# Logits' update as the first step of the next search, the second search held behind the first tokens, and the last block's results copied by ScalarE

## The chip, the cores and the metric

The kernel runs on one core of a Trainium2 chip. The metric is the device time of one execution, in microseconds (us). Engines are named as the profile names them: PE (TensorE), DVE (VectorE), ACT (ScalarE), POOL (GpSimd), SP (SyncE); PEld is PE's weight load. Each engine works through its own queue in order; SP's and POOL's queues also issue the DMA transfers.

## What is computed

Three layers follow one another. Attention with 4 sink positions and a window of 128 gives 3072 tokens of 512 channels. A dense layer (512 to 2048 to 512, with a piecewise quadratic activation) follows. Then each token goes to one of eight experts: all 3072 x 8 logits are taken from the greatest down, and a token takes an expert if the token is free and the expert has fewer than 384 tokens:

```
logits = x @ w_gate
flat = logits.flatten()
order = np.argsort(-flat)
for idx in order:
    tok, e = (int(idx) // E, int(idx) % E)
    if assigned[tok] >= 0 or counts[e] >= cap:
        continue
    assigned[tok] = e
    counts[e] += 1
for e in range(E):
    mask = assigned == e
    h = np.maximum(x[mask] @ w1[e], 0.0)
    out[mask] = h @ w2[e]
```

All matrix work is done in split precision: every operand is a high part (names ending in `h`) and a remainder (ending in `l`), and a product is three matmuls.

## The kernel before, in words

**Stages.** Attention and the dense layer run block by block (256 tokens each) up to about 866 us. The change touches what comes then: routing and the eight experts, and the end of the last block of the dense layer.

**Routing.** The logits stand in one tile `logits` (128 partitions x 24 x 8). Routing goes expert by expert in eight phases (`phase`, L760). A phase finds the expert that fills up first among those left, and its 384 tokens. `prep` (L765) takes each token's greatest logit `v` and its one-hot `own`. `search(r)` (L775), seven rounds, finds the threshold bit by bit: DVE compares `v` with 32 candidate thresholds (`ind`), PE counts (`pg`, copied by DVE as `cnt`, then `pc`), DVE turns the counts into the next candidates (`hit`, `row`, `m`, `th`). `pick` (L822) names the expert (`pe` on PE, `top`, `eid`, `est` on DVE); SP reads `eid` and can then load that expert's weights. `rank` (L854) numbers its tokens and, at its end (L869 to L876), updates the logits for the next phase: the expert found and the tokens taken are set to a very low value (`pe`, `pt`, and two writes of `logits`). `places` (L878) and `tokens` (L896) make one-hots (`oh`), PE adds them up to token numbers (`pk`), ACT and DVE finish them (`tf`, `tok`). `gather` (L944) has POOL issue three indirect transfers that fetch 128 token rows each (`xg`). `turn` (L957) transposes them on PE (`xt`); ACT writes the high part `xsh`, DVE the remainder `xsl`.

**Experts.** `weights` (L919) loads one of four chunks of `w1` and `w2` (SP, buffers `w1r`, `w2r`, four in all), ACT rounds them (`w1h`, `w2h`), and the remainder comes from DVE (`w1l`) or from ACT and an accumulating transfer on POOL's queue (`w2l`). `expert` (L967) has 96 matmuls `hp` (hidden layer, 384 tokens wide) and 72 `us` (output): 168 in all. After each hidden tile ACT writes `hh` and DVE `hl`. ACT copies the outputs (`ot`), POOL scatters them. In what follows, a place in an expert is the number of its 168 matmuls that stand ahead of it in PE's queue.

**What sets the order.** `experts` (L1039) gives every step a planned time; the steps are written in the order of these times, and the tile framework's scheduler puts the instructions of each engine in a fixed order by priority, in which the steps of `find` (prep, searches, pick, rank) rank as urgent (L1031). The instructions wait for one another through semaphores; an engine that waits holds all that is queued behind.

**The last block.** In `moe1_steps` (L601) the last block's outputs are left for after its logits; `done` (L674) copies each half tile from PSUM to `ev`, the low half by ACT, the high half by DVE (L686), and SP stores `ev` to `x2d`, from which the gathers read.

## Time and profile before

| | us |
|---|---|
| median of three runs | 1244.58 (1243.54 to 1244.86) |
| the profiled execution, its own time | 1243.53 |
| its span, first to last instruction | 1241.3 |
| PE busy | 1143.8 (92%) |
| DVE busy | 860.0 (69%) |
| ACT busy | 695.6 (56%) |
| POOL busy | 462.0 (37%) |
| mean granted clock of PE, share of full | 0.965 |

Times in the rows count from the span's start. A row of a timeline gives start, duration, engine, line, operation, tiles and shapes; in brackets how long the engine had been idle before it and who ended that. A row "x5" is five instructions merged. Matmuls overlap their neighbours, so their cost is read from start to start; the chain of waits has that already.

### The profile page before, as it was taken

Reading aid. Unit: us, or ns where it says so; the run is one execution under the profiler, and the core shown is the slowest. Engines: PE = TensorE matmul, PEld = TensorE weight load, DVE = VectorE, ACT = ScalarE, POOL = GpSimd, SP = SyncE. Lnnn points to the kernel's source line nnn. Section 1 sums busy time; section 2 is a strip of 40 time slices with the busy share of each in tenths; the row PEclk is TensorE's granted clock in tenths of the full one; section 3 lists DMA queues with packets and bytes.
Section 4 is the critical chain, followed back from the end, with each engine's and each line's share of the span. In section 5 each row is a group of like instructions: output and inputs, shape, how many; then the busy total and the mean of one; then the engine's idle time right before and its main releaser. Section 6 shows DMA issues by size and latency. Waiting matters only on the chain.

```text
span 1241.3 us, 24035 instructions
## 1 busy us (share of the span) xinstructions
PE 1143.8 (92%) x8444; PEld 1058.0 (85%) x8444; DVE 860.0 (69%) x2637; ACT 695.6 (56%) x1607; POOL 462.0 (37%) x574
## 2 busy tenths in 40 slices
PE   5998988999999999999999999999599999999995
PEld 3778878999999999999999999998478777778894
DVE  7798988677667777666777677656778677775310
ACT  5675557566667666666666666641454344444421
POOL 1245635344444444443445344440221222222210
PEclk9799989999999999999999999999699999999998
DMA  3555322112121112111111112000895577668620
GB/s 93 146 163 160 119 57 65 41 31 58 35 53 32 24 48 59 35 35 35 24 48 40 50 35 53 1 18 2 224 250 164 168 204 205 187 175 242 160 68 29
DMA packets 147715, 112.84 MB, mean 91 GB/s; under 512 B 101888, under 2 KB 126464, under 8 KB 147584
## 3 DMA queue, kind: packets, MB, share of 16 engines
q1 hardware_dynamic: 138992, 81.31, 22.7%
q0 software_dynamic: 8592, 29.89, 10.3%
q8 instruction: 69, 1.13, 0.4%
q14 instruction: 62, 0.51, 0.1%
HBM read 80.76 MB, written 13.11 MB: 76 GB/s over the span
## 4 chain that ended last, share of the span: by engine, by line
PE 40%; issue 11%; DMA 8%; DVE 8%; POOL 6%; ACT 6%; SPq 0%; POOLq 0%; DVEq 0%; ACTq 0%
PE hp L616 12%; PE up L641 12%; DMA w2r<-in_moe_w_dram 5%; PE us L1009 4%; PE hp L983 3%; DMA w2l<-w2r 3%; PE tp L365 2%; PE xp L384 2%; ACT pr L332 1%; ACT u L625 1%; PE sc L327 1%; POOL xa L403 1%; PE sc L328 1%; DVE ks L292 1%; DVE u L624 1%
## 5 line engine op out<-in xcount | busy, mean ns | idle before, releaser
L628 POOL TENSOR_TENSOR gl<-u,gh 128x256 fp32r<-128x256 f32 x192 | 146.5, 763 | 246.7 <-ACT gh L627 207.6
L641 PE MATMUL up<-woh,gl 128*128 128x256 f32 x576 | 169.9, 295 | 0.5 <-POOL gl L628 0.5
L641 PE MATMUL up<-woh,gh 128*128 128x256 f32 x576 | 165.7, 288 | 0.0
L641 PE MATMUL up<-wol,gh 128*128 128x256 f32 x576 | 165.4, 287 | 0.0
L625 ACT ACTIVATE u<-u,half 128x256 f32<-128x256 f32 x192 | 97.6, 509 | 98.5 <-DVE u L624 94.4
L616 PE MATMUL hp<-xh,wil 128*128 128x256 f32 x768 | 132.6, 293 | 4.6 <-ACT xh L404 3.0
L616 PE MATMUL hp<-xl,wih 128*128 128x256 f32 x768 | 127.1, 286 | 0.8 <-POOL xl L405 0.5
L616 PE MATMUL hp<-xh,wih 128*128 128x256 f32 x768 | 125.7, 285 | 0.0
L626 DVE TENSOR_TENSOR u<-hp,u 128x256 f32<-128x256 f32 x192 | 81.0, 422 | 46.7 <-ACT u L625 43.9
L616 PEld LDWEIGHTS hp<-xh,wil 128*128 128x128 f32 x768 | 107.8, 193 | 6.3 <-ACT xh L404 3.6
L641 PEld LDWEIGHTS up<-woh,gl 128*128 128x128 f32 x576 | 111.0, 193 | 1.7 <-POOL gl L628 0.9
L641 PEld LDWEIGHTS up<-woh,gh 128*128 128x128 f32 x576 | 110.8, 192 | 0.0
L641 PEld LDWEIGHTS up<-wol,gh 128*128 128x128 f32 x576 | 110.7, 192 | 0.0
L616 PEld LDWEIGHTS hp<-xl,wih 128*128 128x128 f32 x768 | 107.1, 192 | 1.8 <-POOL xl L405 1.8
L616 PEld LDWEIGHTS hp<-xh,wih 128*128 128x128 f32 x768 | 107.2, 193 | 0.8 <-issue 0.8
L624 DVE TENSOR_SCALAR u<-hp 128x256 f32<-128x256 f32 x192 | 80.8, 421 | 30.0 <-PE hp L616 26.3
L332 ACT ACTIVATE pr<-pr,sm 128x288 f32<-128x288 f32 (+1 forms) x160 | 85.4, 535 | 20.2 <-DVE sm L330 19.8
L627 ACT CAST gh<-u 128x256 fp32r<-128x256 f32 x192 | 77.5, 404 | 32.5 <-DVE u L626 30.2
L941 POOL DMA_DIRECT2D w2l<-w2r x32 | 29.5, 922 | 155.3 <-ACT w2l L939 138.8
L346 POOL TENSOR_TENSOR pr<-pr,sm 128x576 f32<-128x576 f32 x56 | 65.1, 1162 | 54.4 <-DVE sm L338 40.2
L991 DVE SCALAR_TENSOR_TENSOR hl<-hp,hh 128x384 fp32r<-128x384 f32 x64 | 35.4, 553 | 65.3 <-ACT hh L990 65.2
L1009 PE MATMUL us<-w2h,hl 128*128 128x512 f32 x192 | 79.5, 414 | 0.0
(273 smaller groups left out, 3096.6 us busy)
## 6 DMA issues: line engine op xcount, KB each, us to landing
w1r<-in_moe_w_dram SPq DMA_DIRECT2D x32, 512.0 KB, 5.7
w2r<-in_moe_w_dram SPq DMA_DIRECT2D x32, 512.0 KB, 5.3
w2l<-w2r POOLq DMA_DIRECT2D x32, 512.0 KB, 5.6
dr<-in_moe_w_in_dram SPq DMA_DIRECT2D x16, 512.0 KB, 3.8
dr<-in_moe_w_out_dram SPq DMA_DIRECT2D x16, 512.0 KB, 3.8
x2d<-ev SPq DMA_DIRECT2D x26, 256.0 KB, 2.0
kr<-in_k_dram SPq DMA_DIRECT2D x56, 96.0 KB, 2.6
vr<-in_v_dram SPq DMA_DIRECT2D x56, 96.0 KB, 2.2
```

What stands on the lines that cost most here:

```text
L332: nc.scalar.activation(pr, pr, AF.Exp, bias=sm[:, 0, u:u + 1], scale=-1.0, accum_out=sm[:, 1, u:u + 1])
L346: nc.gpsimd.tensor_tensor(out=pr, in0=pr, in1=r.unsqueeze(2).to_broadcast([P, 2, 2 * P + NS]), op=OP.mult)
L616: nc.tensor.matmul(ps, w_[:, k, fs], x_[:, k, :], start=(i == 0 and k == 0), stop=(i == 2 and k == 3))
L624: nc.vector.tensor_scalar(u, ps, -1.0, 1.0, op0=OP.max, op1=OP.min)
L625: nc.scalar.activation(u, u, AF.Square, bias=self.half, scale=0.5)
L626: nc.vector.tensor_tensor(out=u, in0=ps, in1=u, op=OP.max)
L627: nc.scalar.copy(gh, u)
L628: nc.gpsimd.tensor_tensor(out=gl, in0=u, in1=gh.bitcast(F32), op=OP.subtract)
L641: nc.tensor.matmul(o, g_[:, ts], self.w_out_part(w_, f)[:, cs], start=(f == fa and i == 0 and (cs.start > 0 or t == 0)), stop=(f == fz - 1 ...
L983: nc.tensor.matmul(ps, w_[:, k, fs], x_[:, k, :], start=(i == 0 and k == 0), stop=(i == 2 and k == 3))
L991: nc.vector.scalar_tensor_tensor(hl, ps, 0.0, hh.bitcast(F32), op0=OP.max, op1=OP.subtract)
L1009: nc.tensor.matmul(us[j], h_[:, o], w_[:, f % 2, :], start=(f == 0 and i == 0), stop=(f == nf - 1 and i == 2))
```

## The change

Three things. The update of the logits leaves `rank` and becomes a function `retire`, which the next phase's `prep` calls first. For the first phase, the first instruction of `retire` may stand in DVE's queue only behind the last `xsl` of the first tokens (an order, no semaphore). And the last block's high halves are copied by ACT instead of DVE.

```diff
@@ moe1_steps, done
                 nc.scalar.copy(ev[:, :hw], lo)
-                nc.vector.tensor_copy(ev[:, hw:], hi)
-                if not hold:
+                if hold:
+
+                    nc.scalar.copy(ev[:, hw:], hi)
+                else:
+                    nc.vector.tensor_copy(ev[:, hw:], hi)
                     nc.vector.tensor_copy(o, lg)
@@ phase
-    def phase(self, last, out):
+    def phase(self, last, out, before):
...
         def prep():
+            if before:
+                before["retire"]()
...
-            if not last:
-                pt = self.rw.tile([P, GT], F32, name="pt")
-                pe = self.rw.tile([P, E], F32, name="pe")
-                nc.vector.tensor_scalar(pe, st["est"], 2.0 * DEAD, -DEAD, op0=OP.mult, op1=OP.add)
...
+        def retire():
+
+            ge = st["ge"]
+            pt = self.rw.tile([P, GT], F32, name="pt")
+            pe = self.rw.tile([P, E], F32, name="pe")
+            got = nc.vector.tensor_scalar(pe, st["est"], 2.0 * DEAD, -DEAD, op0=OP.mult, op1=OP.add)
+            if not before:
+
+                self.tc.add_manual_dep(got.ins, out["turned"], AFTER, reason="behind the tokens")
...
+        out["retire"] = retire
@@ turn
-        nc.vector.tensor_tensor(out=xl[:, :, o], in0=ps, in1=xh[:, :, o].bitcast(F32), op=OP.subtract)
+        got = nc.vector.tensor_tensor(out=xl[:, :, o], in0=ps, in1=xh[:, :, o].bitcast(F32), op=OP.subtract)
+        cur["turned"] = got.ins.name
@@ experts
-            find, fetch = self.phase(k + 1 == E, curs[k])
+            find, fetch = self.phase(k + 1 == E, curs[k], curs[k - 1] if k else None)
```

`AFTER` is a dependency without a semaphore. The scheduler works the order of all engines out anew, so the instructions move in places that the diff doesn't name. Lines of the changed kernel are 1 to 15 higher than those of the kernel before.

**DVE, first phase, from the one-hots' inputs on.** Before (`ind`, `own`, `cnt`, `hit` are the second search's first round; `v` its prep):

```order
L876 TENSOR_TENSOR logits<-logits,pt 128x192
L885 SCALAR_TENSOR_TENSOR a<-a,z 128x24
L890 TENSOR_TENSOR rr<-bs,t_row 128x3x24
L767 TENSOR_REDUCE v<-logits 128x24
L887 TENSOR_SCALAR ab<-a 128x24
L781 TENSOR_TENSOR ind<-v,pat_11516 128x768
L769 TENSOR_TENSOR own<-logits,v 128x192
L900 TENSOR_TENSOR oh<-slot,ab 128x128x6 x2
L789 CAST cnt<-pg 128x32
L900 TENSOR_TENSOR oh<-slot,ab 128x128x6
L803 TENSOR_SCALAR hit<-pc 128x8
L900 TENSOR_TENSOR oh<-slot,ab 128x128x6
```

In the changed kernel:

```order
L899 SCALAR_TENSOR_TENSOR a<-a,z 128x24
L904 TENSOR_TENSOR rr<-bs,t_row 128x3x24
L901 TENSOR_SCALAR ab<-a 128x24
L914 TENSOR_TENSOR oh<-slot,ab 128x128x6 x4
L923 SCALAR_TENSOR_TENSOR tok<-pk,tf 128x3
L979 TENSOR_TENSOR xsl<-xt,xsh 128x4x128 x3
L881 TENSOR_SCALAR pe<-est 128x8
L887 TENSOR_TENSOR logits<-logits,pe 128x192
L888 TENSOR_TENSOR logits<-logits,pt 128x192
L773 TENSOR_REDUCE v<-logits 128x24
L787 TENSOR_TENSOR ind<-v,pat_11516 128x768
L775 TENSOR_TENSOR own<-logits,v 128x192
```

The one-hots, `tok` and the three `xsl` now stand together; the update and the whole second search stand behind them, among the first expert's `w1l` and `hl`. On PE the second search's pick moves from behind 50 of the first expert's matmuls to behind 126; on POOL the three gathers move ahead of the first `w2l` transfer.

**ACT, from the second expert's first weights to its tokens.** Before:

```order
L990 ACTIVATE hh<-hp 128x384
L935 CAST w1h<-w1r 128x1024
L939 ACTIVATE w2l<-w2r 128x1024
L940 CAST w2h<-w2r 128x1024
L907 COPY tf<-pk 128x3
L935 CAST w1h<-w1r 128x1024
L990 ACTIVATE hh<-hp 128x384
L939 ACTIVATE w2l<-w2r 128x1024
L940 CAST w2h<-w2r 128x1024
L935 CAST w1h<-w1r 128x1024
L990 ACTIVATE hh<-hp 128x384
```

In the changed kernel:

```order
L921 COPY tf<-pk 128x3
L1029 COPY ot<-us 128x512
L949 CAST w1h<-w1r 128x1024
L953 ACTIVATE w2l<-w2r 128x1024
L954 CAST w2h<-w2r 128x1024
L978 CAST xsh<-xt 128x4x128 x2
L949 CAST w1h<-w1r 128x1024
L953 ACTIVATE w2l<-w2r 128x1024
L978 CAST xsh<-xt 128x4x128
L954 CAST w2h<-w2r 128x1024
L1005 ACTIVATE hh<-hp 128x384 x6
```

Before, the first expert's last two `hh` stand between the second expert's late weight casts; in the changed kernel all eight stand ahead of the second expert's first cast, and the late casts stand ahead of that expert's `xsh` instead.

## Rows read from the trace of the kernel before

**Rows 1.** Busy time by stretch: stretch, its length, busy us (count) by engine, clock, DMA.
```profile
866.00:888.00 22.00, 10.04 (x96) 7.74 (x94) 17.72 (x75) 6.42 (x10) 5.07 (x5) 0.61 0.64 171
888.00:938.00 50.00, 46.04 (x286) 38.12 (x287) 36.43 (x123) 27.30 (x36) 12.34 (x12) 0.90 0.86 236
938.00:982.00 44.00, 41.90 (x290) 34.33 (x289) 32.89 (x118) 18.95 (x27) 10.21 (x10) 1.00 0.62 183
...
1157.00:1194.00 37.00, 37.00 (x207) 33.04 (x206) 9.18 (x15) 15.80 (x25) 9.06 (x10) 1.00 0.53 131
```
**Rows 2.** PE's waits, 888 to 1157 us: total us, times, longest.
```profile
PE pg L786 <- DVE ind L781: 6.9, 7, 2.3
PE pc L793 <- DVE cnt L789: 5.7, 6, 1.7
PE po L857 <- DVE tot L852: 2.6, 1, 2.6
```
**Rows 3.** Timeline of DVE, first search to first tokens.
```profile
844.25 0.35 DVE L767 TENSOR_REDUCE v<-logits 128x24 f32<-128x192 f32 x1
...
866.99 0.16 DVE L835 TENSOR_REDUCE top<-sm 128x1 f32<-128x8 f32 x1
...
867.76 0.42 DVE L686 COPY ev<-up 128x256 f32<-128x256 f32 x1
...
871.87 0.43 DVE L876 TENSOR_TENSOR logits<-logits,pt 128x192 f32<-128x192 f32 x1
...
873.97 0.55 DVE L900 TENSOR_TENSOR oh<-slot,ab 128x768 bf16<-128x768 bf16 x1
...
878.71 0.15 DVE L909 SCALAR_TENSOR_TENSOR tok<-pk,tf 128x3 int32<-128x3 f32 x1
```
**Rows 4.** Timeline of ACT, the same stretch.
```profile
867.97 0.65 ACT L685 COPY ev<-up 128x256 f32<-128x256 f32 x2 [23.85 <-PE up L641]
...
873.63 1.03 ACT L940 CAST w1h<-w1r 128x1024 fp32r<-128x1024 f32 x1
...
877.26 0.15 ACT L907 COPY tf<-pk 128x3 f32<-128x3 f32 x1
```
**Rows 5.** Timeline of POOL, the same stretch.
```profile
876.74 0.89 POOL L941 DMA_DIRECT2D w2l<-w2r  x1 [1.55 <-ACT w2l L939]
879.15 1.09 POOL L951 DMA_INDIRECT xg<-x2d,tok  x1 [1.52 <-DVE tok L909]
```
**Rows 6.** DMA issues, 866 to 890 us: queue, count, size, median us to landing.
```profile
x2d<-ev SPq DMA_DIRECT2D x2, 256.0 KB, 4.4
...
w2l<-w2r POOLq DMA_DIRECT2D x1, 512.0 KB, 4.6
```
**Rows 7.** Chain of waits: start, us, what.
```profile
888.09 3.58 PE hp L983 x11
...
896.62 0.47 DVE hl L991
...
919.64 5.65 DMA w2r<-in_moe_w_dram
...
929.77 2.40 PE us L1009 x10
...
943.16 2.46 PE hp L983 x13
```
**Rows 8.** Timeline of PE, the second expert's first matmuls.
```profile
938.40 0.87 PE L983 MATMUL hp<-xsh,w1l 128*128 128x384 f32 x4
```
**Rows 9.** Timeline of DVE, second search.
```profile
890.11 1.23 DVE L936 TENSOR_TENSOR w1l<-w1r,w1h 128x1024 fp32r<-128x1024 f32 x1 [0.16 <-ACT w1h L935]
...
891.87 0.19 DVE L789 CAST cnt<-pg 128x32 f16<-128x32 f32 x1 [0.53 <-PE pg L786]
...
896.44 0.18 DVE L789 CAST cnt<-pg 128x32 f16<-128x32 f32 x1
...
906.37 0.15 DVE L835 TENSOR_REDUCE top<-sm 128x1 f32<-128x8 f32 x1
```

More of the change, by code (lines that the diff above doesn't have):

```diff
@@ L17 @@
 DRAM = bass.MemoryType.DRAM
+AFTER = mybir.DependencyInfo(mybir.DependencyClass.NoSync, mybir.DependencyReason.DATA)
 DEP = mybir.DependencyInfo(mybir.DependencyClass.Sync, mybir.DependencyReason.DATA)
@@ L868, in rank @@
                 nc.vector.tensor_scalar(ge[:, i], z, float(P * i), None, op0=OP.is_gt)
-            if not last:
-                pt = self.rw.tile([P, GT], F32, name="pt")
-                pe = self.rw.tile([P, E], F32, name="pe")
-                nc.vector.tensor_scalar(pe, st["est"], 2.0 * DEAD, -DEAD, op0=OP.mult, op1=OP.add)
-                nc.vector.tensor_tensor(out=pt, in0=ge[:, 0], in1=ge[:, 3], op=OP.subtract)
-                nc.vector.tensor_scalar(pt, pt, 2.0 * DEAD, -DEAD, op0=OP.mult, op1=OP.add)
-                nc.vector.tensor_tensor(out=lm, in0=lm, in1=pe.unsqueeze(1).to_broadcast([P, GT, E]), op=OP.min)
-                nc.vector.tensor_tensor(out=lm, in0=lm, in1=pt.unsqueeze(2).to_broadcast([P, GT, E]), op=OP.min)
+        def retire():
[5 more added lines that the diff above has]
+                self.tc.add_manual_dep(got.ins, out["turned"], AFTER, reason="behind the tokens")
+            nc.vector.tensor_tensor(out=pt, in0=ge[:, 0], in1=ge[:, 3], op=OP.subtract)
+            nc.vector.tensor_scalar(pt, pt, 2.0 * DEAD, -DEAD, op0=OP.mult, op1=OP.add)
+            nc.vector.tensor_tensor(out=lm, in0=lm, in1=pe.unsqueeze(1).to_broadcast([P, GT, E]), op=OP.min)
+            nc.vector.tensor_tensor(out=lm, in0=lm, in1=pt.unsqueeze(2).to_broadcast([P, GT, E]), op=OP.min)
+        out["retire"] = retire
         def places():
```

## The prediction

> **What bounds the kernel now.** I read the views in this order: busy time by stretch, the matrix engine's waits, then the chain and the timelines around the place that the change touches. [Rows 1] cut the end of the program near the first hidden matmul of each expert (of four stretches like that from 938 one stands there): between 866 and 888 us there is almost no matmul work to do, the first expert takes 50 us, the ones after it about 44, and the seventh, beside which no search runs, takes 37. So two things cost time here: the hand-over from routing to the first expert, and what the search for the next expert costs beside each expert. A search's own matmuls are small: seven rounds of count matmuls. The larger part is in [rows 2]: between 888 and 1157 us PE stood still 6.9 us for `ind`, 5.7 us for `cnt` and 2.6 us for `tot`, all made by DVE for the search, 15.2 us together. DVE is late there because it works in order and the search's instructions stand behind `w1l` and `hl`, which wait for weights that are loaded only once the search before has named the expert. PE and DVE are thus tied to the load chain after each pick.
>
> **Term 1, the hand-over.** The pick is known at 866.99 (`top`); the first one-hot `oh` starts only at 873.97 and `tok` at 878.71 [rows 3]. In between DVE did five instructions of the logits' update, the first step and round 0 of the second search, and two 0.42 us copies `ev`; all of these leave that stretch. The first chain alone then needs some 4.5 us from `top` to `oh` and 2.1 us for four `oh`, so the one-hots end near 873.7 and the last six `pk` matmuls near 874.3. ACT is then the last: `tf` stands behind `w1h`, which runs from 873.63 to 874.66, since its weights had to land [rows 4]. `tf` no longer stands behind the `w2` pair, though, as it did at 877.26. So `tok` comes at 874.87, and with the 0.44 us from `tok` to the gather in [rows 3, 5] the first gather starts at 875.3 instead of 879.15. That is 3.8 us earlier. The `w2l` transfer of 876.74 now goes behind the gathers on POOL's queue [rows 5]; it goes out after three gathers, near 880, and with its 4.6 us [rows 6] lands near 885, while the first product that reads it stands 36 matmuls into the expert, after 891, which hides it. The two `ev` halves that move to ACT put four copies where two took 0.65 [rows 4]: the second store goes out about 0.5 us later on SP's queue, and `w2r` behind it; its 4.4 us landing [rows 6] ends by 874.3, 1 us before the gather that waits for it, so I cost it at nothing; without that cover it would cost up to 0.5. The `xsl` remainders no longer wait behind a search's `ind`, 0.4 us. The first hidden matmul moves from 888.09 [rows 7] to 883.9: **4.2 us earlier**.
>
> **Term 2, the first expert with a search inside it.** The second search used to run from 872 to 906.37 [rows 9], its first three rounds inside the hand-over where PE was idle. Now DVE's queue holds it until the third `xsl`, about 884.6. No row shows a search that begins there, so I bound it. Below: the first search, with nothing else on DVE, took 22.7 us from `v` to `top` [rows 3]; with some 0.9 us of the update in front (two `logits` like the 0.43 us one of 871.87, and `pe`) the pick would be at 908.2. But the order puts the pick behind 126 expert matmuls (50 before), 90 `hp` of 0.189 us and 36 `us` of 0.24 us [rows 7], 25.7 us together, which with 1.4 us of slow clock and 2.5 us of count matmuls is not before 913.5. Above: two rounds 4.57 us apart, as between 891.87 and 896.44 [rows 9], in all seven rounds plus 2.2 us give 918.8. I take the first search plus what DVE's order puts inside it, three `w1l` of 1.23 [rows 9] and seven `hl` of 0.47 us [rows 7]: 22.7 + 0.9 + 3.7 + 3.3 = 30.6, a pick at **915.2**, nearest to the row with an expert running. It is 8.8 us later than 906.37.
>
> **Term 3, the gap before the second expert.** From the pick the second expert's tokens need their own path, and in the new order ACT makes the casts of the second expert's `w1h`, `w2l`, `w2h` chunk 3 and half of chunk 4 before its `xsh`. In the kernel before the third `w2r` went out 13.3 us after the pick and landed 5.65 later [rows 7], because its buffer is freed by the first `w2l`. So: 18.9 us to that landing, 0.45 for an `ot` copy now ahead of it, 2.0 for `w2l` and `w2h`, 1.1 for two `xsh`, 1.95 for the next casts and 0.6 for the last `xsh`: 25.0 us. The first expert's 42 matmuls left after the pick last only some 10 us, so PE has nothing for most of the rest. The second expert's first matmul comes at 940.2 instead of 938.40 [rows 8]: **1.8 us later**, terms 1 and 2 included.
>
> PE starts that expert after a pause. After the like pause at 866 to 888 the granted clock was 0.61 of full [rows 1], which mixes the 2.4 GHz before with the 1.2 GHz after, and the first eleven hidden matmuls took 3.58 us, 0.325 each, against 0.189 later [rows 7]. Eleven at that rate cost **1.4 us** more. The Trainium skill, "TensorE: Matmul & The Clock Gate", Part 1, says that the slow clock is the array's default and only activity releases it, which speaks against any change that opens a pause; this case's trace agrees with its 0.325 us. Without that rule, had the clock stayed up, the sum below would end 1.4 us lower.
>
> **Term 4, what later experts give back.** The picks of the third to the seventh search move from 33, 21, 3, -12 and -22 matmuls into an expert to 68, 55, 37, 16 and -2. The load chain of a pick blocks ACT some 19 to 25 us after it. Before, `hh` casts of the running expert stood behind those late casts, so `hl`, and the search's `cnt` behind it on DVE, were late, and PE with them. In the new order the second expert's `hh` all stand ahead of the late casts, the third's all but one. Of the 15.2 us in [rows 2] 11.8 fall after 938. They could all go (-11.8) or, since `cnt` still stands behind late `w1l`, none (0). Of the experts two to five, two lose their `hh` behind late casts, two keep some; I take half, **5.9 us back**. The move of DVE's two copies in the last block saves nothing else: DVE is not waited for there.
>
> **Sum.** +1.8 + 1.4 - 5.9 = -2.7. The profiled execution took 1243.53 us (span 1241.3); it becomes 1240.8. The median of the runs, 1244.58, lies 1.05 above it, so the forecast is 1241.9. Its own range, with the second search one round faster or slower and a third to two thirds given back, is 1238 to 1246.
>
> **Rivals.** *The gap is not paid back (slower).* Each round in the first expert takes the 4.57 us of [rows 9] instead of about 4; the pick is then at 918.8, 3.6 later, and PE pauses as much longer; the second expert, whose rounds are also placed among its matmuls, gives nothing back, so only half of some 7 us returns: 3.2 + 3.6 - 3.4 = +3.4, about 1248. It decides once the second pick is later than about 918. For it: the order ties every round to a number of matmuls, and DVE's queue holds three `w1l` that wait for weights. Against it: the loads of that expert also start 3.6 us earlier. Chance 0.28.
>
> *The late waits vanish (much faster).* If the later picks free PE of all of the 11.8 us, 3.2 - 11.8 = -8.6, about 1236. For it: ACT's order in the second expert; against it: fourth and fifth experts keep `hh` behind late casts. Chance 0.19.
>
> *Earlier start and gap cancel (no change).* The tokens come 4.2 us earlier, the gap takes it, and later experts wait as before, only at other matmuls; or the gathers still wait for the stores and nothing is gained in front. +1.8 at most, 1244 to 1246. Chance 0.09.
>
> **Chances.** The forecast has 0.44, of which 0.27 lies below -0.2%, 0.15 within and 0.02 above; 0.2% is about what a measurement of this kernel can tell from no change. Faster 0.27 + 0.19 = 0.46; within 0.15 + 0.09 = 0.24; slower 0.02 + 0.28 = 0.30. Both signs hold much, so the range reaches over the rivals: 1234 to 1250.
>
> **What would show it.** Right: first gather at 875 to 876, first hidden matmul near 884; second pick 913 to 917; a pause of PE of 10 us or more before the second expert, with a granted clock below 1 there; second expert near 940; experts three to six each 1 to 2 us shorter than before, with less waiting for `ind` and `cnt`. Wrong, if the first gather is not 3 us earlier, if the pick comes after 918, or if PE's waits for DVE after 940 do not fall.

## The result and the profile after

The changed kernel is slower. Its median is 1256.2 us (1251.4 to 1260.2, six runs) against 1244.25 (1240.3 to 1248.8, six runs) for the kernel before, measured beside it; the ratio is 1.0071, with a 95% interval from 1.0043 to 1.0099. The profiled execution took 1254.8 us (span 1253.0, mean granted clock 0.961). Here and below a ratio is of fast runs alone; a run that is over 1.5% above the fastest of its kernel counts as slow, which leaves out five of twelve in experiment 12, the traced one among them, and one each in experiments 9 and 13.

Busy time by stretch, changed kernel, cut at the first hidden matmul of each expert (the columns are those of [rows 1]):

```profile
866.00:885.30 19.30, 7.79 (x58) 6.55 (x56) 8.69 (x36) 7.08 (x12) 5.18 (x5) 0.66 0.69 181
885.30:944.00 58.70, 46.31 (x308) 37.96 (x308) 42.31 (x144) 26.61 (x36) 13.74 (x13) 0.85 0.74 205
944.00:993.00 49.00, 44.71 (x287) 37.04 (x288) 33.39 (x120) 19.42 (x27) 9.94 (x10) 0.93 0.62 167
993.00:1036.60 43.60, 41.91 (x288) 34.42 (x287) 33.04 (x121) 19.17 (x27) 10.54 (x10) 1.00 0.63 181
1036.60:1080.50 43.90, 41.57 (x288) 34.25 (x287) 33.04 (x121) 19.28 (x27) 10.31 (x10) 1.00 0.63 177
1080.50:1126.80 46.30, 43.67 (x289) 35.63 (x288) 33.57 (x122) 19.18 (x27) 9.69 (x10) 0.96 0.62 172
1126.80:1166.40 39.60, 37.74 (x211) 32.96 (x210) 26.04 (x85) 21.84 (x31) 11.37 (x11) 1.00 0.87 248
1166.40:1203.40 37.00, 37.00 (x206) 32.83 (x205) 9.06 (x15) 15.50 (x24) 9.46 (x10) 1.00 0.62 158
```

Against [rows 1]: the hand-over is shorter (19.3 us instead of 22.0), the first expert longer (58.7 instead of 50), and the second longer (49.0 instead of 44) at a lower clock. The seventh takes 37 as before. The same view of the kernel before for the third to sixth expert, which [rows 1] leave out:

```profile
982.10:1027.10 45.00, 42.09 (x289) 34.16 (x288) 32.68 (x122) 18.88 (x27) 9.69 (x10) 1.00 0.63 178
1027.10:1070.60 43.50, 41.44 (x279) 34.22 (x278) 33.37 (x124) 19.18 (x27) 10.81 (x10) 1.00 0.65 177
1070.60:1115.10 44.50, 42.12 (x280) 34.01 (x278) 33.98 (x131) 19.99 (x28) 9.85 (x10) 1.00 0.73 201
1115.10:1156.70 41.60, 38.98 (x208) 34.42 (x209) 22.10 (x56) 21.20 (x30) 10.77 (x11) 0.96 0.83 240
```

PE's waits of the changed kernel from 885 to 1167 us, which answer to [rows 2]:

```profile
PE xt L976 <- DMA xg<-x2d,tok: 8.8, 2, 7.7
PE pc L799 <- DVE cnt L795: 6.7, 3, 3.1
PE pg L792 <- DVE ind L787: 5.5, 5, 2.6
...
PE po L863 <- DVE tot L858: 1.7, 1, 1.7
```

The waits for `cnt`, `ind` and `tot` are not gone: 13.9 us instead of 15.2. New is the first row, a wait of 7.7 us for the second expert's gather. The chain of waits of the changed kernel shows where it stands (start, us, what):

```profile
915.90 0.17 DVE top L841
...
929.84 9.07 DMA xg<-x2d,tok
...
943.97 2.29 PE hp L998 x6
...
974.50 9.81 DMA w1r<-in_moe_w_dram
```

The second pick is known at 915.90; the second expert's first gather goes out at 929.84, its rows are there 9.07 us later, and the second expert starts at 943.97. The last row is from inside the second expert and is taken up below.

**How far one trace can be trusted.** The first pick comes at 867 us in both traces shown so far, but between 860 and 870 in those that follow, from earlier stages that no edit touches. So times are counted from the first pick below. Both kernels were traced twice, in us:

| | first hidden matmul of the first expert | second pick | second expert | experts two to six together | last matmul |
|---|---|---|---|---|---|
| before, two traces | 21.1, 21.2 | 39.4, 39.9 | 71.4, 75.7 | 218.3, 217.6 | 359.6, 363.3 |
| changed, two traces | 18.1, 18.1 | 48.7, 48.4 | 76.8, 76.0 | 222.4, 225.2 | 369.2, 371.1 |

The means differ by -3.0, +8.9, +2.8, +5.9 and +8.7 us. The last is about the measured loss: 0.71% of 1244 is 8.8 us. It is the sum of +2.8, the later start of the second expert, and +5.9, what experts two to six take longer. The kernel before differs from itself by 4.3 us in the second expert's start and by 3.7 us at the last matmul, so the +2.8 is within what two traces can differ by; the sum of +8.7 and the +5.9 are not.

### The profile page after: what moved, and what is told of

The parts are those of the page before. It is cut to its first block, busy times and chain, and to the rows that moved or that the text cites. A ratio compares the mean times of both kernels' runs of the same rounds, so it can differ in the third digit from the quotient of the medians.

```text
span 1253.0 us, 24041 instructions
## 1 busy us (share of the span) xinstructions
PE 1144.7 (91%) x8444; PEld 1061.1 (85%) x8444; DVE 859.6 (69%) x2635; ACT 695.8 (56%) x1609; POOL 463.7 (37%) x574
## 3 DMA queue, kind: packets, MB, share of 16 engines
q0 software_dynamic: 8592, 29.89, 10.4%
## 5 line engine op out<-in xcount | busy, mean ns | idle before, releaser
L347 POOL TENSOR_TENSOR pr<-pr,sm 128x576 f32<-128x576 f32 x56 | 65.0, 1160 | 55.9 <-DVE sm L339 42.9
L1005 ACT ACTIVATE hh<-hp 128x384 fp32r<-128x384 f32 x64 | 31.2, 490 | 95.0 <-PE hp L998 82.7
```

Of the source, the lines that this page charges most:

```text
L347: nc.gpsimd.tensor_tensor(out=pr, in0=pr, in1=r.unsqueeze(2).to_broadcast([P, 2, 2 * P + NS]), op=OP.mult)
L1005: nc.scalar.activation(hh, ps, AF.Relu)
```

## The experiments

Each was timed beside the kernel before; a ratio below 1 is faster than that, and the interval behind it is 95%.

**Experiment 1: the search not held.**

```diff
-            if not before:
-
-                self.tc.add_manual_dep(got.ins, out["turned"], AFTER, reason="behind the tokens")
```

> The change without its middle part: the second search is not held; the update is still called by the next prep and ACT still copies the last block's high halves. In this kernel the instructions of all engines stand in the same order as if ACT's copies alone had been put into the kernel before, so the move of the update by itself moves nothing. The second pick stands behind 67 of the first expert's matmuls (before 50, changed kernel 126), the later ones behind 55, 37, 16, -2 (before 33, 21, 3, -12). Theory (the hold is the loss: it takes the second search out of the hand-over): pick at 905 to 909 us, first expert's first hidden matmul near 887.5, second's at 938 to 941, and 1242 to 1246 us, within 0.3% of before. Rival 1 (ACT's copies cost): the first gather comes later than 879, and a good part of the 12 us loss stays, 1249 or more. Rival 2 (term 4 of the prediction, picks at later places free PE of its late waits): experts two to five 1 us or more shorter each than before, 1237 to 1240 us.

Measured: 1241.8 us, ratio 0.9949 (0.9922 to 0.9977). Counted from the first pick, the first expert starts at 20.4, the second pick comes at 37.1 and the second expert starts at 68.5 us. The loss is gone, and what stays of the change is a small gain. By the scheduler's order the move of the update alone moves no instruction, so the gain is put down to ACT's copies (no run has them alone): DVE has two instructions less in the hand-over and the pick comes 2.6 us earlier. The trace does not show the gain: its last matmul comes at 361.4 us, between the two of the kernel before, and it is of the slowest of the twelve runs (1246.8 us). Against the changed kernel's second measurement (1.0074, below) the hold costs 1.0074 / 0.9949 = 1.3%. Rival 1 falls. Rival 2 falls by the trace: experts two to six took 223.0 us. That is as long as in the changed kernel (222.4 and 225.2), though nothing is held here.

**Experiment 2: held, but DVE makes the copies.**

```diff
-                if hold:
-
-                    nc.scalar.copy(ev[:, hw:], hi)
-                else:
-                    nc.vector.tensor_copy(ev[:, hw:], hi)
+                nc.vector.tensor_copy(ev[:, hw:], hi)
+                if not hold:
                     nc.vector.tensor_copy(o, lg)
```

> The change without ACT's copies: the last block's high halves stay with DVE, the search is held as in the changed kernel (pick behind 126 matmuls). Theory (the hold is the loss): pick at 914 to 918 us, second expert's first hidden matmul 942 to 946, 1253 to 1258 us, like the changed kernel. Rival (ACT's copies are a good part of the loss, through the second store that goes out later): first gather 0.5 us earlier or more than in the changed kernel's 875.9, second expert before 941, under 1250 us.

Measured: 1260.1 us, 1.0085 (1.0051 to 1.0119). The first gather is 8.7 us after the first pick, as in the changed kernel, the second pick 51.6, the second expert 79.2 us. With the hold, ACT's copies are worth nothing that can be measured; the loss is the hold's.

**Experiment 3: held behind `tok` only.**

```diff
-                self.tc.add_manual_dep(got.ins, out["turned"], AFTER, reason="behind the tokens")
+                self.tc.add_manual_dep(got.ins, out["named"], AFTER, reason="behind the tokens")
...
-                nc.vector.scalar_tensor_tensor(out["tok"], pk[:, 3:6], float(P), tf, op0=OP.mult, op1=OP.add)
+                got = nc.vector.scalar_tensor_tensor(out["tok"], pk[:, 3:6], float(P), tf, op0=OP.mult, op1=OP.add)
+                out["named"] = got.ins.name
```

> The changed kernel with the second search held behind the token numbers (tok) instead of the last xsl: it may start some 9 us earlier, beside the gathers, while PE is still idle. Order: pick behind 93 matmuls (changed kernel 126, before 50). Theory (the second expert starts some 28 to 32 us after the second pick, whatever the start of the first): tok near 875 and the first expert's first hidden matmul near 885.4 as in the changed kernel, pick 906 to 909, second expert's first hidden matmul 935 to 940, 1240 to 1246 us. Rival (every search that stands among the first expert's matmuls loses the same): pick 912 or later, second expert 942 or later, 1250 us or more.

Measured: 1246.4 us, 1.0000 (0.9973 to 1.0026). First expert 18.0, second pick 41.2, second expert 68.5 us after the first pick: as the theory has it. So the early hand-over is kept and the second expert starts as in experiment 1, yet by the times 0.5% is lost against it: the start of the second expert isn't the whole of this hold's cost. Where the rest lies the traces do not settle. Experts two to six took 225.7 us, the second alone 49.6, but 223.0 in experiment 1 and 224.8 in experiment 8, which has experiment 1's order; and this trace is of one of the fastest of its twelve runs (1240.5 us).

**Experiment 4: the second expert's `w2l` transfer of chunk 2 behind its gathers.**

```diff
-                nc.gpsimd.dma_start(l.bitcast(F32), r, accum_op=OP.add)
+                acc = nc.gpsimd.dma_start(l.bitcast(F32), r, accum_op=OP.add)
+                if cur["k"] == 1 and c == 1:
+                    self.tc.add_manual_dep(acc.ins, cur["gathers"][-1], AFTER, reason="behind the gathers")
```

(`cur["k"]` is the expert's number, counted from 0.)

> The changed kernel, but the second expert's w2l transfer of chunk 2 goes out on POOL's queue behind that expert's three gathers (in the changed kernel 1.2 us ahead of them). The gap from the second pick to the second expert was 28.1 us where 25.0 was forecast; in it the first gather took 9.1 us from issue to the first transpose, against 5.1 for the first expert's. Theory (the gathers share their queue with w2l): 9.1 falls to 5 to 7 us, the second expert starts 1.5 to 3 us earlier (941 to 942.5), and the time falls by 1 to 3 us against the changed kernel unless the later loads take it back. Rival (the gathers compete with the weight loads of SP's queue): 8 us or more, second expert at 943 to 945, time as the changed kernel.

Measured: 1251.8 us, 1.0034 (1.0006 to 1.0061), 0.4% under the changed kernel, with intervals that overlap. POOL's timeline and PE's, this kernel:

```profile
926.68 1.04 POOL L967 DMA_INDIRECT xg<-x2d,tok  x1 [0.73 <-DVE part L821]
...
930.24 1.02 POOL L955 DMA_DIRECT2D w2l<-w2r  x1
```
```profile
933.02 1.11 PE L978 MATMUL xt<-ident,xg 128*128 128x128 f32 x4 [4.38 <-DMA xg<-x2d,tok]
```

From the first gather's issue to the first transpose it is 6.3 us instead of 9.1 in the changed kernel, and the second expert starts 25.6 us after the second pick instead of 28.1. A `w2l` transfer that goes out 1.2 us ahead of the gathers thus costs them 2.8 us here. In the other traces with the same hold it is 8.1 us (the changed kernel again) and 8.4 (experiment 2), with that transfer 1.2 us ahead. It is not so everywhere: in experiment 5, where nothing is held, it is 5.9 us with the transfer 1.2 us ahead.

**Repeats of both kernels**, unchanged; their numbers are in the table above.

> The changed kernel once more, for a second trace. Theory (the loss stands at two places, the idle time before the second expert and the second expert itself): counted from the first pick, the first expert's first hidden matmul at 17.5 to 18.5 us, the second pick at 48 to 52, the second expert at 75 to 80, its length 47 to 50 us; experts three to six together 173 to 181 us; ratio to the kernel before 1.006 to 1.012. Rival (the sizes of the one trace are chance): second expert under 74 us after the first pick, or its length under 46.

> The kernel before once more, for a second trace. Theory: counted from the first pick, the first expert's first hidden matmul at 20.5 to 21.5 us, the second pick at 38.5 to 41, the second expert at 70 to 73 and 43 to 46 us long; experts three to six together 173 to 179 us. If these four experts differ by several us between the two traces, differences of that size between kernels are no evidence for term 4.

Measured: the changed kernel 1253.8 us, 1.0074 (1.0045 to 1.0102); the kernel before, one run, 1247.2. The theory's bounds held for the changed kernel but for one that concerns a single expert: the second expert took 45.9 us, under the rival's 46, and the third 48.3. For the kernel before, the second expert came at 75.7, outside 70 to 73: its first expert took 54.5 us instead of 50.3. So 4 us in one expert of one trace are no evidence, while the sum over experts two to six differed by 0.7 and 2.8 us between repeats.

**Experiment 5: `hh` and `hl` as urgent as the search** (on experiment 1).

```diff
-            nc.scalar.activation(hh, ps, AF.Relu)
-            nc.vector.scalar_tensor_tensor(hl, ps, 0.0, hh.bitcast(F32), op0=OP.max, op1=OP.subtract)
+            with tc.high_priority(offset=HP):
+                nc.scalar.activation(hh, ps, AF.Relu)
+                nc.vector.scalar_tensor_tensor(hl, ps, 0.0, hh.bitcast(F32), op0=OP.max, op1=OP.subtract)
```

> The first experiment's kernel (search not held), with ACT's and DVE's work on a hidden tile (hh, hl) as urgent as the search, so that hh stands ahead of late weight casts wherever the scheduler can place it. Picks stay where they were in the first three experts (68, 55, 38 against 67, 55, 37). Theory (term 4's mechanism: PE's waits for ind and cnt come from hl, which waits for hh behind late casts): the waits after the second expert's start fall by half or more and the time is 2 to 5 us under the first experiment's. Rival (casts and hl change places at a few points only and the next thing in DVE's queue, w1l behind its load, takes the wait over): within 0.2% of the first experiment.

Measured: 1244.2 us, 0.9971 (0.9946 to 0.9996). No gain over experiment 1. Experts two to six took 217.9 us, but the first took 54.3 with a new wait, `xt` for `xsl`, of 3.7 us.

**Experiment 6: late `w1l` made by transfers instead of DVE** (on experiment 1).

```diff
-            if name == "w1" and (c or not first):
+            if name == "w1" and (c or not first) and not (not first and c > 1):
```

> The first experiment's kernel with the remainder w1l of the last two chunks of the second to eighth expert made as w2l is: ACT writes the negative, POOL's queue adds the weights by an accumulating transfer. DVE loses two 1.23 us instructions per expert that wait for late loads; ACT gains two of 1.0, POOL's queue two transfers of 512 KB. Theory (cnt and ind wait behind w1l): PE's waits for cnt and ind fall by 3 us or more over experts two to six, 2 to 6 us under the first experiment's time. Rival (the load chain itself is the limit: buffers come free only after the slower accumulating transfer, and the gathers share their queue): the first experiment's time or up to 10 us more.

Measured: 1253.2 us, 1.0057 (1.0031 to 1.0083): the rival, 1.1% over experiment 1. PE's waits for `ind` from the second expert on rose to 12.2 us, one of them 6.2.

**Experiments 7 and 8: eight, or four, matmuls of constants behind the first `pk`** (on experiment 1).

```diff
+        if j == 0 and cur["k"] == 0:
+            for i in range(8):
+                mm = nc.tensor.matmul(ps.rearrange("p k c -> p (k c)"), self.one,
+                                      self.slot.rearrange("p a b -> p (a b)")[:, :512], start=True, stop=True)
+                if i == 0:
+                    self.tc.add_manual_dep(mm.ins, cur["placed"], AFTER, reason="behind the places")
```

> The first experiment's kernel (no hold, ACT's copies) with eight matmuls of constants on PE behind the first phase's last pk, into the tile that the first transposes overwrite; PE waits for the gathers there anyway. They shift the scheduler's plan so that the picks stand where they stood in the kernel before: behind 50, 33, 21, 3 matmuls, -12, -22 (first experiment: 67, 55, 37, 16, -2, -14). So this kernel differs from the first experiment in the places, and from the kernel before in the hand-over. Theory (later places do not free PE, they cost: they put cnt and ind behind hl and w1l that come later, with longer single waits and a lower granted clock after them): experts two to six together 216 to 220 us after 223 in the first experiment's trace, time 2 to 6 us under the first experiment's, 0.990 to 0.994 of before. Rival (term 4 of the prediction: later places help): 2 us or more over the first experiment. Rival 2 (the places do not matter): the same as the first experiment within 0.2%, experts two to six differ by less than 3 us.

> The same with four matmuls in place of eight: the order then is that of the first experiment (67, 55, 37, 16, -2), so this is the control for the eight matmuls themselves. Theory: the time of the first experiment within 0.2%, the first expert's first hidden matmul 20 to 21 us after the first pick. Rival (matmuls of constants keep the granted clock up and that is what helps): the first eleven hidden matmuls take under 3 us in place of 3.58, and 1 us or more under the first experiment.

Measured: eight (places of the kernel before) 1243.9 us, 0.9987 (0.9962 to 1.0012); four (places of experiment 1) 1240.8 us, 0.9961 (0.9930 to 0.9992). The intervals overlap; if anything, the earlier places are the worse by 0.26%. So the theory that later places cost falls, and term 4's opposite isn't shown either. The traces show an exchange: with the earlier places experts two to six took 220.1 us and with the later ones 224.8, but the second expert started at 73.7 and at 69.1 us, and the last matmul came at 363.8 and 363.9. The first nine hidden matmuls behind the four constants took 3.05 us, 0.34 each, no less than the 0.325 of the kernel before.

**Experiment 9: experiment 4's edit for experts two to eight, the search not held** (on experiment 1).

```diff
-                nc.gpsimd.dma_start(l.bitcast(F32), r, accum_op=OP.add)
+                acc = nc.gpsimd.dma_start(l.bitcast(F32), r, accum_op=OP.add)
+                if cur["k"] and c == 1:
+                    self.tc.add_manual_dep(acc.ins, cur["gathers"][-1], AFTER, reason="behind the gathers")
```

> The first experiment's kernel with the w2l transfer of chunk 2 behind the gathers for experts two to eight (the fourth experiment did so for the second expert in the changed kernel and was 0.4% under it). Theory (the gathers' landing only counts where PE waits for it, which it does in the held kernels alone): no gain, within 0.3% of the first experiment, or slower, since buffers come free later. Rival (earlier rows help every expert): 2 us or more under the first experiment.

Measured: 1230.5 us, 0.9881 (0.9845 to 0.9916): the rival, and the fastest kernel of this study. Busy time by stretch, its experts two to six:

```profile
928.90:973.00 44.10, 41.95 (x289) 34.48 (x288) 33.30 (x121) 18.97 (x27) 10.49 (x10) 1.00 0.69 195
973.00:1016.10 43.10, 41.62 (x289) 34.34 (x288) 33.05 (x121) 19.02 (x27) 10.37 (x10) 1.00 0.65 181
1016.10:1059.10 43.00, 42.02 (x289) 34.35 (x288) 33.36 (x121) 19.17 (x27) 9.81 (x10) 1.00 0.66 184
1059.10:1100.70 41.60, 41.11 (x281) 33.81 (x280) 33.33 (x126) 19.07 (x27) 9.79 (x10) 1.00 0.71 194
1100.70:1142.20 41.50, 38.80 (x209) 33.72 (x208) 24.25 (x71) 22.47 (x31) 10.72 (x11) 0.96 0.80 233
```

PE's waits, its experts two to six (929 to 1142 us), and then those of experiment 1 (937 to 1160 us):

```profile
PE pg L792 <- DVE ind L787: 4.6, 5, 1.9
PE po L863 <- DVE tot L858: 2.4, 1, 2.4
PE pc L799 <- DVE cnt L795: 0.3, 1, 0.3
```
```profile
PE pc L799 <- DVE cnt L795: 7.4, 4, 2.9
PE pg L792 <- DVE ind L787: 3.7, 6, 2.1
PE po L863 <- DVE tot L858: 1.8, 1, 1.8
...
```

The waits for `cnt` fell from 7.4 to 0.3 us, and the granted clock is 1.00 in four of the experts two to six (three in experiment 1). PE's order is the same in both kernels, DVE's and ACT's but for three exchanges of neighbours; what comes sooner is the last of an expert's four `w1h` casts, on which `w1l` and so `cnt` wait: 19.9 to 21.3 us after the pick (experts two to six) instead of 21.8 to 23.4, though its load goes out no sooner. That cast stands in ACT's queue behind the `w2` casts of chunk 3, whose load is now faster. SP's and ACT's timelines in the third expert's weights, experiment 9 and then experiment 1:

```profile
954.61 0.37 SPq L938 DMA_DIRECT2D w2r<-in_moe_w_dram  x1
958.83 1.06 ACT L950 ACTIVATE w2l<-w2r 128x1024 fp32r<-128x1024 f32 x1 [1.89 <-DMA w2r<-in_moe_w_dram]
```
```profile
964.32 0.37 SPq L938 DMA_DIRECT2D w2r<-in_moe_w_dram  x1
970.68 1.06 ACT L950 ACTIVATE w2l<-w2r 128x1024 fp32r<-128x1024 f32 x1 [4.38 <-DMA w2r<-in_moe_w_dram]
```

From the load's issue to ACT's use it is 4.2 us here and 6.4 in experiment 1; over experts two to six 3.9 to 4.3 and 5.4 to 6.3. In experiment 1 the `w2l` transfer of chunk 2 goes out 11.3 to 12.4 us after the pick, just ahead of this load (13.6 to 14.8); in experiment 9 it goes out at 17.9 to 19.6, when the load has landed. So the edit helps, as far as these traces show, by keeping the large transfer away from the weights that the chain waits for, and not through the gathers, for which PE did not wait inside experts two to six of experiment 1 either. That the transfer itself slows the load was not tested apart.

**Experiment 10: experiment 5 for experts two to eight alone** (on experiment 1).

```diff
+            with tc.high_priority(offset=HP if cur["k"] else 0):
```

> The fifth experiment (hh and hl urgent) for experts two to eight alone; the first expert's order is that of the first experiment. Theory (hh behind late casts is a part of the longer experts two to six): experts two to six together 217 to 221 us, 1 to 5 us under the first experiment's time. Rival (in one trace chance; another instruction takes the wait over): within 0.2% of the first experiment.

Measured: 1238.9 us, 0.9947 (0.9918 to 0.9977), experts two to six 220.0 us. The same as experiment 1.

**Experiments 11 to 14: experiment 9's edit on other kernels**: on the kernel before (11), on the changed kernel (12), on experiment 3 (13) and on experiment 10 (14). **Experiment 15** is experiment 9 once more.

> The kernel before with one edit: the w2l transfer of chunk 2 goes out behind the gathers for experts two to eight, as in the ninth experiment, and nothing of the change. Theory (the gain of the ninth experiment is this edit's and stands apart from the change): cnt no longer holds PE, experts two to six together 208 to 215 us, 1231 to 1237 us, 0.988 to 0.993 of before. Rival (it needs the search places that ACT's copies bring): 0.995 of before or more.

> The changed kernel, hold included, with the same edit for experts two to eight. Against the ninth experiment it differs by the hold alone. Theory A (the hold's loss stands in the pause before the second expert and in the slow clock after it; the longer experts two to six come from waits that this edit removes): the second expert starts 72 to 75 us after the first pick (66.3 in the ninth experiment), experts two to six together 213 to 218, 1237 to 1243 us, some 7 to 11 us over the ninth experiment. Theory B (the late search keeps costing in every later expert): experts two to six together 221 or more, 1246 us or more. Theory C (with the gathers early the hold costs nothing): within 3 us of 1230.5.

> The third experiment (search held behind tok only) with the same edit. Theory A: first expert 18 us after the first pick, second pick 41, second expert 66 to 68 us after the first pick, 1229 to 1234 us, about the ninth experiment's time. Rival (a search held at all costs in the experts that follow, as in the third experiment's 49.6 us for the second expert): 1236 us or more.

> The ninth experiment's kernel with hh and hl as urgent as the search for experts two to eight. Theory (what is left of PE's waits, 9.5 us, stands behind hl and hh in part): 1 to 4 us under the ninth experiment. Rival (the places hardly change): within 0.3% of it.

> The ninth experiment's kernel once more (search not held, ACT's copies, w2l of chunk 2 behind the gathers for experts two to eight). Theory (its gain is of the edit): ratio 0.985 to 0.992 of before; counted from the first pick, second expert at 65 to 68 us, experts two to six together 211 to 217 us with a granted clock of 1.00 in at least four of the five. Rival (chance of one chip or trace): 0.994 or more, experts two to six 219 us or more.

Measured: (11) 0.9941 (0.9921 to 0.9961), experts two to six 215.9 us, so less than the theory's gain; (12) 1.0002 (0.9966 to 1.0039), and the median of all its twelve runs 1252.7 us, 0.4% above the kernel before; (13) 0.9974 (0.9952 to 0.9996); (14) 0.9918 (0.9887 to 0.9948); (15) 1232.8 us, 0.9904 (0.9873 to 0.9935), second expert 68.0 us after the first pick, experts two to six 212.2 us. The edit is worth 0.6% on the kernel before, and on experiment 1 0.7% (0.9881 / 0.9949) or 0.5% (0.9904 / 0.9949). The hold costs 1.2% with the edit (1.0002 / 0.9881; by the repeat 1.0%) as it did without. By its time (12) is theory B, in which the late search goes on costing behind the second expert's start; its trace (second expert at 77.0 us, then 223.6) is of a run of 1254.0 us, longer than every run in the ratio, and is not used for more. (13) shows it better: its second expert starts at 67.8 us, as in experiments 9 and 15 (66.3 and 68.0), but experts two to six then took 220.1 us against 213.3 and 212.2, and the time is 0.7 to 0.9% longer. Experiment 14 gives nothing beyond experiment 9.

## Why the prediction was wrong

**Term 1 was right in kind, 1.2 us too large.** Forecast: gather at 875.3, first hidden matmul 4.2 us earlier, at 883.9. The timelines of DVE, ACT and POOL of the changed kernel, which answer to [rows 3 to 5]:

```profile
867.21 0.16 DVE L841 TENSOR_REDUCE top<-sm 128x1 f32<-128x8 f32 x1
...
875.15 0.16 DVE L923 SCALAR_TENSOR_TENSOR tok<-pk,tf 128x3 int32<-128x3 f32 x1 [1.00 <-ACT tf L921]
...
886.92 0.35 DVE L773 TENSOR_REDUCE v<-logits 128x24 f32<-128x192 f32 x1
```
```profile
874.03 1.03 ACT L954 CAST w1h<-w1r 128x1024 fp32r<-128x1024 f32 x1
874.97 0.15 ACT L921 COPY tf<-pk 128x3 f32<-128x3 f32 x1
```
```profile
874.46 1.15 POOL L955 DMA_DIRECT2D w1l<-w1r  x1 [31.59 <-ACT w1l L953]
875.90 1.07 POOL L965 DMA_INDIRECT xg<-x2d,tok  x1 [0.30 <-issue]
```

`tf` did stand behind `w1h`, and `tok` came 0.3 us later than forecast; the gather came 0.75 behind `tok`, not 0.44: POOL was issuing a `w1l` transfer until 875.61. From the gather's issue to the first transpose it was then 5.1 us in both traces, where the kernel before has 3.8 and 3.9, a step that the forecast took as unchanged. The first expert started at 885.35, 3.0 us earlier counted from the first pick.

**Term 2 was right.** The pick was forecast at 915.2 and came at 915.90, behind 126 matmuls. The search inside the first expert is no slower than the one it replaces: 29.0 us from `v` (886.92) to `top`, 33.9 before (872.45 to 906.37). It starts late, and that is all.

**Term 3 had the wrong waiter and 3 us too little.** The forecast let the second expert wait for ACT, whose weight casts stand ahead of `xsh`, 25.0 us after the pick. ACT was not last:

```profile
937.76 1.03 ACT L954 CAST w2h<-w2r 128x1024 fp32r<-128x1024 f32 x1
940.10 0.58 ACT L978 CAST xsh<-xt 128x512 fp32r<-128x512 f32 x1 [1.32 <-PE xt L976]
```

ACT idled 1.32 us for the transposes, and PE for the gather, whose landing the forecast had not counted as a step: the `w2l` transfer stood just ahead of it on POOL's queue (experiment 4). The gap was 28.1 us, and between 25.6 and 28.1 in every kernel with a held search. Against the two traces of before the second expert started 2.8 us later, where 1.8 was forecast, so this step mis-sized the sum by little. Against the one trace that the forecast was made from it is 5.4 us; that the error looks small is in part the luck of the second trace.

The slow clock was sized right. Busy time by stretch at the second expert's start:

```profile
944.00:946.00 2.00, 2.00 (x6) 2.00 (x7) 1.93 (x5) 0.86 (x1) 0.61 (x1) 0.50 0.51 100
946.00:948.00 2.00, 2.00 (x14) 1.84 (x14) 0.06 (x1) 0.00 (x0) 0.00 (x0) 0.66 0.83 164
948.00:950.00 2.00, 2.00 (x16) 1.84 (x16) 1.33 (x7) 0.49 (x1) 0.00 (x0) 1.00 0.03 8
```

Half of 2 us and a third of 2 us are 1.7 us, where 1.4 was forecast.

**Term 4 is the step that failed**: "half, 5.9 us back" over the later experts. With the 1.4 us of slow clock, the forecast had experts two to six 4.5 us shorter; the two traces of each kernel have them 5.9 us longer. These 10.4 us and the 1.0 us of term 3 are the whole error of the sum (-2.7 forecast, +8.7 to the last matmul). Two things were wrong in the term.

First, the waits were not freed. (Of the waits of [rows 2] 11.5 us fall after 938, not 11.8, which matters little.) All of PE's waits in experts two to six were 13.6 and 14.7 us in the changed kernel's traces and 12.0 and 11.2 before. The term rested on ACT's order, above all on the second expert's `hh`, which all stand ahead of late casts. There the search then waited for `w1l` instead: one wait for `cnt` of 3.1 us, behind a `w1l` whose load took 9.81 us (the chain's last row above). In the fifth expert `hl` behind a late `hh` came back: `w2l` had to wait for its load on ACT, `hh` stood behind it, `hl` and the search's `cnt` behind that. DVE in the second expert, and ACT and DVE in the fifth:

```profile
985.41 1.23 DVE L950 TENSOR_TENSOR w1l<-w1r,w1h 128x1024 fp32r<-128x1024 f32 x1 [4.63 <-ACT w1h L949]
```
```profile
1104.18 1.06 ACT L953 ACTIVATE w2l<-w2r 128x1024 fp32r<-128x1024 f32 x1 [3.59 <-DMA w2r<-in_moe_w_dram]
...
1105.65 0.56 DVE L1006 SCALAR_TENSOR_TENSOR hl<-hp,hh 128x384 fp32r<-128x384 f32 x1 [2.83 <-ACT hh L1005]
```

Second, the term had no price for what a wait does to the clock. Around one wait of the changed kernel, PE's timeline, and then the stretches behind it:

```profile
1103.56 0.39 PE L1024 MATMUL us<-w2h,hh 128*128 128x512 f32 x1
1106.36 0.24 PE L799 MATMUL pc<-cnt,pile 128*128 128x8 f16 x4 [2.41 <-DVE cnt L795]
...
1110.15 0.63 PE L1024 MATMUL us<-w2l,hh 128*128 128x512 f32 x1
1110.58 0.63 PE L1024 MATMUL us<-w2h,hh 128*128 128x512 f32 x1
```
```profile
1106.30:1108.00 1.70, 1.64 (x12) 1.64 (x12) 1.22 (x8) 1.26 (x3) 1.00 (x2) 0.93 0.75 149
1108.00:1110.00 2.00, 2.00 (x12) 1.69 (x12) 1.97 (x4) 0.41 (x1) 1.39 (x3) 0.50 0.87 158
1110.00:1112.00 2.00, 2.00 (x11) 1.39 (x10) 0.70 (x3) 0.08 (x1) 0.71 (x1) 0.70 0.78 264
...
```

After 2.41 us without a matmul the clock is at 0.50, the level of 1.2 GHz, from about 1108 to 1111, and two `us` matmuls stand 0.43 us apart instead of 0.23. That costs 0.07 x 1.7 + 0.5 x 2 + 0.3 x 2 = 1.7 us beside the wait itself. The Trainium skill, "TensorE: Matmul & The Clock Gate", Part 1, "HAM oscillation — how this bites in real kernels", tells of a kernel whose waits for data between groups of matmuls throttle the array again and again. This trace agrees in kind, with its 0.50 behind a wait for DVE, though this wait is shorter than those that the page tells of. In the nineteen traces of this study the granted clock fell 46 times inside experts two to six, each time during a wait of PE of more than 1 us or within 1.6 us behind it; 48 other waits of more than 1 us were followed by no fall.

Adding both up accounts for the differences between these traces. Lost to the clock is the sum over experts two to six of length x (1 - granted clock), from the stretches as shown above (changed kernel: 49.0 x 0.07 + 46.3 x 0.04 = 5.3):

| experts two to six, us | together | PE's waits | lost to the clock | the rest |
|---|---|---|---|---|
| before, two traces | 218.3, 217.6 | 12.0, 11.2 | 1.7, 1.8 | 204.6, 204.6 |
| changed, two traces | 222.4, 225.2 | 13.6, 14.7 | 5.3, 8.7 | 203.5, 201.8 |
| experiment 1 | 223.0 | 14.5 | 3.7 | 204.8 |
| experiment 8 (experiment 1's order) | 224.8 | 14.1 | 7.4 | 203.3 |
| experiment 13 | 220.1 | 11.2 | 5.0 | 203.9 |
| experiments 9, 15 | 213.3, 212.2 | 7.6, 6.4 | 1.7, 1.7 | 204.0, 204.1 |

The rest is nearly the same everywhere, within 5 us over all nineteen traces (a wait that falls into the slow time counts twice, hence the lower ones). Of the changed kernel's 5.9 us, 2.6 are waits and 5.3 the clock; the rest takes 2 back. Of the 5.3, some 1.7 are the slow clock at the second expert's start, which the forecast had at 1.4; the others it had at nothing.

**The rivals.** The outcome is that of the first, the gap not paid back, but not by its mechanism: it was to decide where the pick comes later than 918, and the pick came at 915.9. The other two are excluded by the result.

**What stays open.** That the hold is the loss is shown (experiments 1 and 2). Where it acts is shown in part. Against experiments 1 and 8, which are not held and have ACT's copies, the changed kernel's second expert starts 7.6 us later (76.8 and 76.0 against 68.5 and 69.1), and experts two to six take as long (222.4 and 225.2 against 223.0 and 224.8): there the hold's cost is the late start. So the longer later experts, on which term 4 failed, are not the hold's alone. Against the kernel before, experiments 1 and 8 have them too, together with a second expert that starts 4.8 us sooner; experiment 7, with the places of the kernel before, is nearer to that kernel in both (220.1 us and a start at 73.7). Only beside experiment 9's edit are the later experts clearly longer with a hold, in the one trace of experiment 13. Why they are longer is only argued: in experiment 1 the picks stand behind 67, 55, 37 and 16 matmuls of experts one to four, in the changed kernel behind 126 and then 68, 55, 37 and 16 of experts two to five, so one more expert has a search with all its rounds inside. It was not tried to fill PE's waits with matmuls inside the experts, which would part the clock's share from the waits'.

## What to carry to other kernels

An engine that idles while data is fetched is free room for the next phase's chain; holding that chain back to start the present phase 3 us earlier took the room away and cost some 1.2%. An expected gain from waits that go must be read at every place where they stand, not at the first one, and each wait priced with the time at the slow clock behind it. It can pay to send out a large transfer that is needed late behind the transfers on which the chain waits: that one order, not part of the change, was worth 0.5 to 0.7% here, at least as much as the one part of the change that helped.

## What the runs showed of the hardware that was not expected

- The granted clock was at 0.50 soon after a single wait of 2.41 us in the middle of an expert, while behind a wait of 2.32 us in the kernel before (until 1011 us) it stayed at 1.00. In the second trace of the kernel before the same wait, 2.33 us, was followed by a clock of 0.50, and behind one of 3.10 us in experiment 8 (until 1129 us) it stayed at 1.00: the length of the wait alone did not decide it. The extra loss, 1.7 us, is nearly as large as the wait.
- An accumulating transfer of 512 KB that went out on POOL's queue 1.2 us ahead of the gathers made the first gather's rows arrive 9.1 us after its issue instead of 6.3; the same transfer just ahead of a weight load (experiment 1) went with 5.4 to 6.3 us from that load's issue to its use, instead of 3.9 to 4.3 (experiment 9).
- In PE's hand-over, 5.1 us passed from the first gather's issue to the first transpose in the changed kernel (875.90 to 880.98) and 3.8 before (879.15 to 882.92), though the gather had been moved ahead of `w2l`. In the changed kernel a `w1l` transfer went out 1.4 us ahead of it, before a `w2l` transfer 2.4 us.
